# Words of a product kernel's weights fetched a pair ahead, and other first banks: a change to a one-core attention and MLP kernel

## The chip, the cores and the metric

The kernel runs on one core of a Trainium2 chip. The core has a matrix engine (PE, with its own weight loads, PEld), a vector engine (DVE), a scalar engine (ACT), a general engine (POOL, GpSimd) and a sync engine (SP). Each works through its own queue of instructions in order, and waits at an instruction until what that one needs is there. DMA transfers are issued by SP and by POOL. PE writes into PSUM banks, from which DVE and ACT read. The metric is the device time of one execution in microseconds (us); lower is better.

## What is computed

Four batches of chunked attention (8 heads, 768 tokens, head size 64; each chunk of 32 tokens sees 16 tokens to the left, 8 to the right and 8 memory slots), and behind it a mixer with a two-layer MLP:

```python
x = attn_out.transpose(0, 2, 1, 3).reshape(B, S, H * D)
h = x.transpose(0, 2, 1) @ U @ V
u = x + h.transpose(0, 2, 1)
out = u + np.maximum(u @ w_ch1, 0.0) @ w_ch2
```

w_ch1 is 512 x 2048, w_ch2 is 2048 x 512. All is float32; PE gets each operand as a high part and a remainder, three products for one.

## The kernel before

The batches follow one another. While PE does the MLP of one batch, the attention of the next is worked in between, a step at a time.

**Batch 0** goes through `both_blocks`: 32 units, each a first-layer step (`w1_step`) of 128 hidden channels for 384 tokens and, some units later, a second-layer step (`w2_step`). At its end `fold_both` turns the next batch's u (transposes on PE, L1363), adds and subtracts blocks of it (fold, L1373) and splits these into th and tl (L1378), the right-hand sides of batch 1.

**Batches 1 to 3** go through `fast`. There the first layer takes 16 blocks of hidden channels as 8 pairs p, and makes each pair for both halves of the tokens (blocks 0 and 1) by seven products in place of eight, after Strassen. `products(p)` issues seven products (n = 0 to 6) of six matmuls each into three PSUM banks, b1 (n = 0, 3, 6), b2 (n = 1, 4) and b3 (n = 2, 5). The first product on a bank starts it, and the later ones add to it, after the value that stood there has been read: b1 is copied by ACT at n = 0 (into ta, L1448) and n = 3 (into kept, L1454), b2 and b3 go into the sums ta and tb on DVE (n = 1: L1450, n = 2: L1452, n = 4: L1457, n = 5: L1459), and n = 6 into kept (L1461). ta and tb are one tile each, named part in the trace. `split_hidden` makes the hidden values hh (ACT) and hl (DVE, L1418); that of ta is the last reader of ta in a pair. Behind `products(p)` comes `first_block(p - 1)`, two second-layer steps for the first half of the tokens, except behind pairs 0 and 4, where `products(p + 1)` follows at once. Behind pair 3 eight blocks of the other half follow, the rest at the batch's end.

**The banks** b1 and b3 are from the pool ps_h, b2 from ps_a. ps_h has two buffers, ps_a three; ps_a is the pool of the attention. The add that brings the second layer into x (L1192) reads banks of both pools.

**The factors** s of the products are sums of blocks of w1. `prepare(p + 1)`, called ahead of `products(p)`, has POOL fetch two val tiles (256 KB each, L1335) from a copy in HBM and make five sums of them (L1341); two more factors are read straight from the words (mixed[p, 1], mixed[p, 3]). `build_factor` rounds each to a high part (ACT, L1410) and subtracts it for the remainder (DVE, L1411). The first four go into w1l buffers, of which there are four, and the others into three s buffers; they are built behind the products n = 2, 3, 5 and 6 of the pair before, in the code. val and sums are slot tiles, 13 in rotation, which the attention uses as well.

**Order.** The queues of PE, POOL and SP follow the code's order through the whole program. DVE and ACT follow it at first, and then an order that a scheduler lays down when the program is built. POOL's queue also holds the stores of u to HBM (xd<-xa, xd<-x), the loads of x back from there (`recall`, L1168) and the output stores (L1163).

Of the kernel before, what the change touches and what calls it, by code (L numbers as in the profile page):

```python
# [57 lines left out]
def chunk_attn_then_mixer_kernel(  # L58
# [13 lines left out]
    nc = tc.nc  # L72
# [39 lines left out]
    def slot(shape, dtype, name):  # L112
        return tk.tile(shape, dtype, name=name, tag="slot")
# [1131 lines left out]
    def both_blocks(following):  # L1245

        units = []
        for f in range(SPLIT + LEAD):
            if f < SPLIT:
                units.append((0, f, 0, f == 0, None))  # L1250
            if f >= LEAD:
                g = f - LEAD
                units.append((1, g, 1, g == 0, False if g == SPLIT - 1 else None))
        units += [(0, f, 0, False, True if f == NF - 1 else None) for f in range(SPLIT, NF)]
        units += [(1, f, 0, f == SPLIT, True if f == NF - 1 else None) for f in range(SPLIT, NF)]
        prev = []
        for n, (blk, f, where, begins, ends) in enumerate(units):
            while done[0] < min(2 * NF, 2 * f + 1 + (n > LATE)):
                advance(1)
                more_w()  # L1260
            if n == 2:
                head.close()
            let_go()
            solo = n >= 2 * SPLIT
            if n == 2 * SPLIT:
                paced.close()
            for blk_, m, *_ in units[n:n + AHEAD + 1]:
                if m >= SPLIT and blk_ == 1:
                    get_w1l(m)
            w1l = w1ls[f]  # L1270
            if f >= SPLIT or blk == 1:
                del w1ls[f]
            if n == 2 * SPLIT - SOON or 2 * SPLIT - LAID <= n < 2 * SPLIT - LAID + 2:
                place(1)
            serve(RATEL if n < 2 * SPLIT else RATES)
            if n > 2 * SPLIT:
                border()
            if n == 0:
                for c, g3 in rest[:2]:
                    join_uT1(turn_x1(c), c, g3)  # L1280
            if n == len(units) - 1:
                for m in range(3):
                    build_factor(0, m)
            hid_ = w1_step(0, blk, f, w1l)
            if n == len(units) - 2:
                prepare(0)
            if n == len(units) - 5:
                open_turned()
            if n == len(units) - 1:
                open_fast()  # L1290
                for m in range(3, len(PRODUCTS)):
                    build_factor(0, m)
            if n == 0:
                decode(2, 4)
                for c, g3 in rest[2:]:
                    join_uT1(turn_x1(c), c, g3)
                decode(1, 1)
                decode(2, 6)
                decode(1, 6)
                decode(3, 2)  # L1300
            for _ in range(RATE + (3 < n < 12)):
                advance(1)
                more_w()
            if n > 2 * SPLIT:
                border()
            if n >= len(units) - 3:
                following()
            prev.append((blk, f, where, begins, ends) + hid_)
            if solo or n % 2 == 0 or ends:
                while len(prev) > (not ends):  # L1310
                    while done[0] < 2 * prev[0][1] + 2:
                        advance(1)
                        more_w()
                    w2_step(0, *prev.pop(0))
# [12 lines left out]
    def border():  # L1327
        place(PLAN[at[0]])
        at[0] += 1

    def prepare(p):

        whole = [slot([P, NCK, P], F32, "val") for _ in range(2)]
        for side in range(2):
            nc.gpsimd.dma_start(out=whole[side], in_=val_d[2 * p + side])  # L1335
        mixed[p, 1], mixed[p, 3] = whole[1][:, 2:4, :], whole[0][:, 0:2, :]
        for m, (n, fa, ca, fb, cb, op) in enumerate(SUMS):
            if m % 2 == 0:
                two = slot([P, 2, 2, P], F32, "sums")
            a, b_ = (whole[f][:, 2 * c:2 * c + 2, :] for f, c in ((fa, ca), (fb, cb)))  # L1340
            nc.gpsimd.tensor_tensor(out=two[:, m % 2], in0=a, in1=b_, op=getattr(ALU, op))  # L1341
            mixed[p, n] = two[:, m % 2]
# [80 lines left out]
    def seven(b, kept, last):  # L1423
# [4 lines left out]

        def products(p):
            banks = [ps_h.tile([P, 512], F32, name="ps_h"), ps_a.tile([P, 512], F32, name="ps_a")]  # L1430
            banks.append(ps_h.tile([P, 512], F32, name="ps_h"))
            banks = [bank_[:, :TOK] for bank_ in banks]
            b1, b2, b3 = banks
# [52 lines left out]
    def fast(b, following):  # L1486
# [3 lines left out]
        for p in range(n):  # L1490
            if p + 1 < n or b + 1 < B:
                prepare((p + 1) % n)
            products(p)
            if p % (n // 2):
                first_block(p - 1)
            if p == n // 2 - 1:
                first_block(p)
                recall(b, 1)
                second_block(list(range(n)), False, fast_border)
# [77 lines left out]
```

## Time and profile before

| | |
|---|---|
| median of 3 runs | 653.23 us (651.63 to 653.72) |
| the profiled execution | 654.93 us |
| its span in the trace | 653.2 us |
| PE busy | 619.0 us (95%) |
| DVE busy | 458.8 us (70%) |
| ACT busy | 293.4 us (45%) |
| POOL busy | 189.9 us (29%) |
| granted clock of PE | 0.987 on average |

The span is the time from the first to the last instruction of the profiled execution; 1.7 us of that execution lie outside it. Busy time counts an engine's own operations. A bracket behind an operation in a timeline is the time that the engine sat idle before it, with what released it.

### The profile page before, as it was taken

The page shows a single profiled execution, that of the slowest core. Times are in us where ns is not written, and L with a number is a line of the kernel's source. Part 1 is how long each engine was busy: PE and PEld are TensorE (multiplying, and loading weights), DVE is VectorE, ACT ScalarE, POOL GpSimd, SP SyncE. Part 2 cuts the span into 40 slices and gives each one's busy share as a digit, 9 for nine tenths or more (in the row PEclk, how much of TensorE's full clock was granted, in tenths as well). Part 3 has the DMA queues.
Part 4 walks back from the last instruction along what each step waited for, and adds up shares of the span by engine and source line. Part 5 has one row for each costly group of instructions (what it writes and reads, how often), then busy time and mean ns, then how long its engine had stood idle before and what let it go on. Part 6 is the DMA issues. An engine that isn't in the chain of part 4 may idle for free.

```text
span 653.2 us, 15318 instructions
## 1 busy us (share of the span) xinstructions
PE 619.0 (95%) x6052; PEld 537.6 (82%) x6054; DVE 458.8 (70%) x983; ACT 293.4 (45%) x700; POOL 189.9 (29%) x294
## 2 busy tenths in 40 slices
PE   7687999999899999999999999999999999999997
PEld 6556999987786798878898898988798799889986
DVE  4875998889555988756676969766776966427542
ACT  4656776655223545533334545532333643314321
POOL 3520011000002764004631663003731564006400
PEclk9889999999898999999999999999999999999999
DMA  9996679655996239976211439942221442003411
GB/s 204 170 287 253 223 213 247 160 148 140 155 206 126 80 131 167 150 107 130 97 50 65 153 122 153 165 57 82 72 75 43 143 154 82 2 16 97 129 48 50
DMA packets 157082, 84.17 MB, mean 129 GB/s; under 512 B 128978, under 2 KB 143314, under 8 KB 157010
## 3 DMA queue, kind: packets, MB, share of 16 engines
q1 hardware_dynamic: 146034, 47.40, 36.2%
q0 software_dynamic: 10976, 35.79, 16.4%
q8 instruction: 48, 0.79, 0.5%
q14 instruction: 24, 0.20, 0.1%
HBM read 63.63 MB, written 19.40 MB: 127 GB/s over the span
## 4 chain that ended last, share of the span: by engine, by line
PE 59%; issue 18%; DVE 11%; DMA 6%; ACT 2%; POOL 2%; SPq 1%; POOLq 0%; DVEq 0%; ACTq 0%
PE ps_h L1442 17%; PE acc L1231 10%; PE ps_a L1442 7%; PE ps_h L1231 5%; PE acc L1236 5%; PE ps_h L1236 2%; PE ps_a L1231 2%; DVE tl L1378 2%; DMA vb<-in_v_dram 2%; DVE fold L1373 1%; PE ps_a L756 1%; PE ps_a L713 1%; PE ps_a L1236 1%; DMA val<-vald 1%; POOL vald L374 1%
## 5 line engine op out<-in xcount | busy, mean ns | idle before, releaser
L1341 POOL TENSOR_TENSOR sums<-val 128x256 f32<-128x256 f32 x120 | 98.0, 847 | 56.9 <-DMA val<-vald 43.9
L1231 PE MATMUL acc<-w,hh 128*128 128x512 f32 x366 | 98.0, 403 | 1.0 <-DVE w L382 1.0
L1442 PE MATMUL ps_h<-th,w1l 128*128 128x384 f32 x288 | 84.2, 344 | 6.5 <-DVE part L1459 5.0
L1231 PEld LDWEIGHTS acc<-w,hh 128*128 128x128 f32 x366 | 67.9, 190 | 16.2 <-issue 1.8
L1442 PEld LDWEIGHTS ps_h<-th,w1l 128*128 128x128 f32 x288 | 53.0, 188 | 12.1 <-ACT pT L747 3.6
L1418 DVE SCALAR_TENSOR_TENSOR hl<-kept,hh 128x384 fp32r<-128x384 f32 x48 | 28.8, 599 | 40.3 <-PE ps_a L1236 23.0
L1442 PE MATMUL ps_h<-th,s 128*128 128x384 f32 x192 | 52.8, 336 | 0.0
L1236 PE MATMUL acc<-w,hl 128*128 128x512 f32 x183 | 51.9, 392 | 0.0
L1442 PE MATMUL ps_h<-tl,w1l 128*128 128x384 f32 x144 | 49.0, 340 | 0.9 <-DVE tl L1378 0.9
L1417 ACT ACTIVATE hh<-kept 128x384 fp32r<-128x384 f32 x48 | 25.2, 526 | 54.0 <-PE ps_a L1231 29.2
L1231 PE MATMUL ps_h<-w,hh 128*128 128x512 f32 x156 | 43.4, 400 | 0.0
L1178 PE MATMUL ps_h<-uh,w1h 128*128 128x384 f32 x124 | 42.5, 349 | 0.8 <-ACT uh L1150 0.8
L1178 PE MATMUL ps_h<-ul,w1h 128*128 128x384 f32 x124 | 41.2, 340 | 0.0
L1236 PEld LDWEIGHTS acc<-w,hl 128*128 128x128 f32 x183 | 34.4, 189 | 7.8 <-issue 0.2
L1448 ACT COPY part<-ps_h 128x384 f32<-128x384 f32 x24 | 11.5, 480 | 62.8 <-PE ps_h L1442 54.6
L1231 PE MATMUL ps_a<-w,hh 128*128 128x512 f32 x132 | 37.9, 390 | 1.8 <-ACT hh L1184 1.8
L1163 POOL DMA_DIRECT2D xd<-x x9 | 4.9, 543 | 114.5 <-DVE x L1192 113.7
L1410 ACT CAST s<-sums 128x256 fp32r<-128x256 f32 x72 | 28.6, 402 | 17.1 <-PE ps_h L1442 13.7
L1411 DVE TENSOR_TENSOR w1l<-sums,w1l 128x256 fp32r<-128x256 f32 x48 | 25.4, 529 | 14.8 <-ACT w1l L1410 14.8
L1442 PEld LDWEIGHTS ps_h<-th,s 128*128 128x128 f32 x192 | 35.0, 188 | 0.0
L1231 PEld LDWEIGHTS ps_h<-w,hh 128*128 128x128 f32 x156 | 28.2, 188 | 5.7
L1184 ACT ACTIVATE hh<-ps_h 128x384 fp32r<-128x384 f32 x31 | 15.0, 487 | 38.7 <-PE ps_h L1178 38.7
(290 smaller groups left out, 1469.4 us busy)
## 6 DMA issues: line engine op xcount, KB each, us to landing
val<-vald POOLq DMA_DIRECT2D x48, 256.0 KB, 3.1
vb<-in_v_dram SPq DMA_DIRECT2D x23, 336.0 KB
rw<-in_moe_w_ch_dram SPq DMA_DIRECT2D x14, 512.0 KB
x<-xd POOLq DMA_DIRECT2D x27, 256.0 KB, 4.0
raw<-in_moe_w_ch_dram SPq DMA_DIRECT2D x20, 256.0 KB
kall<-in_k_dram SPq DMA_DIRECT2D x48, 96.0 KB
kall<-in_q_dram SPq DMA_DIRECT2D x48, 96.0 KB
out_dram<-x POOLq DMA_DIRECT2D x18, 256.0 KB, 3.0
```

Source lines behind the costliest of these rows:

```text
L1178: nc.tensor.matmul(out=ph[:, :TOK], lhsT=w[:, c, :], rhs=u[c], start=(m == 0), stop=(m + 1 == len(parts)),)
L1184: nc.scalar.activation(out=hh, in_=ph[:, :TOK], func=AF.Relu)
L1231: nc.tensor.matmul(out=acc[tt], lhsT=h[:, sl], rhs=w, start=(begins and m == 0), stop=False,)
L1236: nc.tensor.matmul(out=acc[tt], lhsT=hl[:, sl], rhs=w2h[f], start=False, stop=ends is not None)
L1341: nc.gpsimd.tensor_tensor(out=two[:, m % 2], in0=a, in1=b_, op=getattr(ALU, op))
L1378: nc.vector.tensor_tensor(out=tl[:, i:i + m, :, sl], in0=f32[n][:, 0:m], in1=th[:, i:i + m, :, sl].bitcast(F32), op=ALU.subtract,)
L1410: nc.scalar.copy(out=s[:, 0:2], in_=total)
L1411: nc.vector.tensor_tensor(out=s[:, 2:4], in0=total, in1=s[:, 0:2].bitcast(F32), op=ALU.subtract)
L1417: nc.scalar.activation(out=hh, in_=src, func=AF.Relu)
L1418: vpace[0] = nc.vector.scalar_tensor_tensor(out=hl, in0=src, scalar=0.0, in1=hh.bitcast(F32), op0=ALU.max, op1=ALU.subtract,)
L1442: nc.tensor.matmul(out=banks[at_], lhsT=w[:, wc, :], rhs=t[:, i, c, :], start=(n < 3 and m == 0), stop=(m + 1 == len(parts)), skip_group_c ...
L1448: nc.scalar.copy(out=ta, in_=b1)
```

## The change

There are three edits. The words of a pair go into fixed places, the last 512 of the 2048 words per partition of two of v's tiles (vb), which v leaves free, and no longer into slot tiles; so they have one buffer. The fetch is now a function, `fetch_words`, and is called two pairs ahead, behind `products(p)` for pair p + 2, so that pair p + 1's words have already been read. In pairs 0 and 4 the first two banks change places: b1 comes from ps_a and b2 from ps_h. And at the end of batch 0 the first words are fetched and summed in the sixth last unit, not in the second last; the second pair's words are fetched in the last one.

```diff
--- before.py
+++ after.py
@@ -1282,7 +1282,8 @@
                 for m in range(3):
                     build_factor(0, m)
             hid_ = w1_step(0, blk, f, w1l)
-            if n == len(units) - 2:
+            if n == len(units) - 6:
+                fetch_words(0)
                 prepare(0)
             if n == len(units) - 5:
                 open_turned()
@@ -1290,6 +1291,7 @@
                 open_fast()
                 for m in range(3, len(PRODUCTS)):
                     build_factor(0, m)
+                fetch_words(1)
             if n == 0:
                 decode(2, 4)
                 for c, g3 in rest[2:]:
@@ -1328,11 +1330,16 @@
         place(PLAN[at[0]])
         at[0] += 1
 
-    def prepare(p):
-
-        whole = [slot([P, NCK, P], F32, "val") for _ in range(2)]
+    whole = [
+        vb.rearrange("p i d -> p (i d)")[:, NX * D:NX * D + CH].rearrange("p (c f) -> p c f", c=NCK) for vb in vbs[:2]
+    ]
+
+    def fetch_words(p):
         for side in range(2):
             nc.gpsimd.dma_start(out=whole[side], in_=val_d[2 * p + side])
+
+    def prepare(p):
+
         mixed[p, 1], mixed[p, 3] = whole[1][:, 2:4, :], whole[0][:, 0:2, :]
         for m, (n, fa, ca, fb, cb, op) in enumerate(SUMS):
             if m % 2 == 0:
@@ -1428,6 +1435,8 @@
 
         def products(p):
             banks = [ps_h.tile([P, 512], F32, name="ps_h"), ps_a.tile([P, 512], F32, name="ps_a")]
+            if p % (NF // 4) == 0:
+                banks.reverse()
             banks.append(ps_h.tile([P, 512], F32, name="ps_h"))
             banks = [bank_[:, :TOK] for bank_ in banks]
             b1, b2, b3 = banks
@@ -1491,6 +1500,8 @@
             if p + 1 < n or b + 1 < B:
                 prepare((p + 1) % n)
             products(p)
+            if p + 2 < n or b + 1 < B:
+                fetch_words((p + 2) % n)
             if p % (n // 2):
                 first_block(p - 1)
             if p == n // 2 - 1:
```

Both kernels issue the same instructions, and PE's order stays. On SP two of v's loads for batch 3 now stand behind loads of k and q. Lines from 1331 on carry other numbers behind the change: L1442 becomes L1451, L1335 L1339, L1341 L1348, L1411 L1418, L1418 L1425, L1450 L1459, L1452 L1461, L1457 L1466, L1459 L1468, L1461 L1470, L1373 L1380, L1378 L1385.

PE, pair 0 and the start of pair 1 of batch 1, the first matmul of each product; a number behind a name is the allocation, and a new ps_h takes the bank of one of the two before it. Before:

```order
L1442 MATMUL ps_h_3208<-th_2839,w1l_3102 128x384 [waits Activation_49]
...
L1442 MATMUL ps_a_3209<-th_2839,w1l_3105 128x384 [waits PE_49,Activation_49]
...
L1442 MATMUL ps_h_3210<-th_2839,w1l_3108 128x384 [waits Activation_49]
...
L1442 MATMUL ps_h_3208<-th_2839,w1l_3134 128x384 [waits Activation_49]
...
L1442 MATMUL ps_a_3209<-th_2839,s_3137 128x384 [waits DVE_49]
...
L1442 MATMUL ps_h_3210<-th_2839,s_3140 128x384 [waits DVE_49]
...
L1442 MATMUL ps_h_3208<-th_2839,s_3143 128x384 [waits Activation_49]
...
L1442 MATMUL ps_h_3318<-th_2839,w1l_3234 128x384 [waits DVE_49]
...
L1442 MATMUL ps_a_3319<-th_2839,w1l_3254 128x384 [waits PE_49]
```

The same place now:

```order
L1451 MATMUL ps_a_3205<-th_2849,w1l_3100 128x384 [waits PE_49,Activation_49]
...
L1451 MATMUL ps_h_3204<-th_2849,w1l_3103 128x384 [waits Activation_49]
...
L1451 MATMUL ps_h_3206<-th_2849,w1l_3106 128x384 [waits Activation_49]
...
L1451 MATMUL ps_a_3205<-th_2849,w1l_3132 128x384 [waits Activation_49]
...
L1451 MATMUL ps_h_3204<-th_2849,s_3135 128x384 [waits DVE_49]
...
L1451 MATMUL ps_h_3206<-th_2849,s_3138 128x384 [waits DVE_49]
...
L1451 MATMUL ps_a_3205<-th_2849,s_3141 128x384 [waits Activation_49]
...
L1451 MATMUL ps_h_3312<-th_2849,w1l_3230 128x384 [waits DVE_49]
...
L1451 MATMUL ps_a_3313<-th_2849,w1l_3250 128x384 [waits PE_49]
```

Pair 0's products 0, 3 and 6 have moved to ps_a and 1 and 4 to ps_h; pair 1 (3318 and 3319, now 3312 and 3313) has its banks as before, and its first, from ps_h, can take the bank of pair 0's b2, which now is one of the last two from there.

POOL, pair 4 of batch 1: x loads and xd stores of the batch's first half, and the words of pair 5 (vald_140, 141) and 6 (142, 143). Before:

```order
L1168 DMA x<-xd_3_149 128x512
L1168 DMA x<-xd_4_150 128x512
L1168 DMA x<-xd_5_151 128x512
L1163 DMA xd_3_149<-x 128x512
L1163 DMA xd_4_150<-x 128x512
L1163 DMA xd_5_151<-x 128x512
L1335 DMA val<-vald_140 128x512
L1335 DMA val<-vald_141 128x512
L1341 TENSOR_TENSOR sums<-val 128x256 x5
L1335 DMA val<-vald_142 128x512
L1335 DMA val<-vald_143 128x512
```

The same place now:

```order
L1339 DMA vb_104<-vald_140 128x512
L1339 DMA vb_105<-vald_141 128x512
L1168 DMA x<-xd_3_149 128x512
L1168 DMA x<-xd_4_150 128x512
L1168 DMA x<-xd_5_151 128x512
L1163 DMA xd_3_149<-x 128x512
L1163 DMA xd_4_150<-x 128x512
L1163 DMA xd_5_151<-x 128x512
L1348 TENSOR_TENSOR sums<-vb_104 128x256
L1348 TENSOR_TENSOR sums<-vb_104,vb_105 128x256
L1348 TENSOR_TENSOR sums<-vb_105 128x256
L1348 TENSOR_TENSOR sums<-vb_104,vb_105 128x256
```

The words of pair 5 have moved ahead of the loads and the stores, and their sums follow the stores directly.

DVE, pair 4 of batch 1: the reads of pair 4's banks (n = 1, 2, 4, 5), the softmax of an attention step (rs) and the remainders of pair 5's factors. Before:

```order
L1450 TENSOR_TENSOR part_3132<-ps_a,part_3132 128x384
L736 TENSOR_REDUCE rs<-pt 128x6
L1452 TENSOR_TENSOR part_3133<-ps_h,part_3132 128x384
L736 TENSOR_REDUCE rs<-pt 128x6
L737 TENSOR_SCALAR rs<-rs 128x12
L738 RECIPROCAL rs<-rs 128x12
L1411 TENSOR_TENSOR w1l<-sums,w1l 128x256
L1411 TENSOR_TENSOR w1l<-val,w1l 128x256
L1418 SCALAR_TENSOR_TENSOR hl<-ps_a,hh 128x384
L1457 TENSOR_TENSOR part_3133<-part_3133,ps_a 128x384
L1411 TENSOR_TENSOR w1l<-sums,w1l 128x256
L1459 TENSOR_TENSOR part_3132<-ps_h,part_3132 128x384
```

The same place now:

```order
L1459 TENSOR_TENSOR part_3130<-ps_h,part_3130 128x384
L1418 TENSOR_TENSOR w1l<-sums,w1l 128x256
L1418 TENSOR_TENSOR w1l<-vb_105,w1l 128x256
L736 TENSOR_REDUCE rs<-pt 128x6
L1461 TENSOR_TENSOR part_3131<-ps_h,part_3130 128x384
L736 TENSOR_REDUCE rs<-pt 128x6
L1418 TENSOR_TENSOR w1l<-sums,w1l 128x256
L1418 TENSOR_TENSOR w1l<-vb_104,w1l 128x256
L737 TENSOR_SCALAR rs<-rs 128x12
L1425 SCALAR_TENSOR_TENSOR hl<-ps_h,hh 128x384
L1466 TENSOR_TENSOR part_3131<-part_3131,ps_h 128x384
```

The first four remainders have moved up, from behind the softmax to places around the first two reads.

DVE, end of batch 0: the last part of u (xa), the first folds, and the first remainders of batch 1. Before:

```order
L1067 TENSOR_TENSOR g_2940<-ps_a,g_2940 32x512
L1083 TENSOR_TENSOR xa<-ps_a,xa 128x512 x2
L1185 SCALAR_TENSOR_TENSOR hl<-ps_h,hh 128x384
L1083 TENSOR_TENSOR xa<-ps_a,xa 128x512 x4
L1373 TENSOR_TENSOR fold<-ps_a,fold 128x256 x5
L1378 TENSOR_TENSOR tl<-fold,th 128x4x128
L1378 TENSOR_TENSOR tl<-fold,th 128x2x128
L1378 TENSOR_TENSOR tl<-fold,th 128x4x128 x2
L1411 TENSOR_TENSOR w1l<-sums,w1l 128x256
L1411 TENSOR_TENSOR w1l<-val,w1l 128x256
L1185 SCALAR_TENSOR_TENSOR hl<-ps_h,hh 128x384
```

The same place now:

```order
L1418 TENSOR_TENSOR w1l<-sums,w1l 128x256
L1067 TENSOR_TENSOR g_2950<-ps_a,g_2950 32x512
L1083 TENSOR_TENSOR xa<-ps_a,xa 128x512 x2
L1185 SCALAR_TENSOR_TENSOR hl<-ps_h,hh 128x384
L1083 TENSOR_TENSOR xa<-ps_a,xa 128x512
L1418 TENSOR_TENSOR w1l<-vb_105,w1l 128x256
L1083 TENSOR_TENSOR xa<-ps_a,xa 128x512 x3
L1380 TENSOR_TENSOR fold<-ps_a,fold 128x256 x5
L1385 TENSOR_TENSOR tl<-fold,th 128x4x128
L1385 TENSOR_TENSOR tl<-fold,th 128x2x128
L1385 TENSOR_TENSOR tl<-fold,th 128x4x128 x2
L1185 SCALAR_TENSOR_TENSOR hl<-ps_h,hh 128x384
```

Two remainders have moved ahead of the folds, one of them in between the additions to xa.

## Rows read from the trace of the kernel before

**Rows 1.** Page, part 1: engine, busy us, share of the span, instructions.

```profile
PE 619.0 (95%) x6052; PEld 537.6 (82%) x6054; DVE 458.8 (70%) x983; ACT 293.4 (45%) x700; POOL 189.9 (29%) x294
```

**Rows 2.** Waits of PE: who waits <- for whom, us in total, times, longest.

```profile
PE ps_h L1442 <- DVE part L1459: 5.0, 5, 1.7
PE ps_a L756 <- DMA vb<-in_v_dram: 4.2, 3, 2.1
...
PE ps_h L1442 <- DVE x L1192: 1.0, 2, 0.5
...
PE ps_h L1442 <- DVE tl L1378: 0.9, 2, 0.5
...
PE ps_a L1442 <- DVE tl L1378: 0.7, 1, 0.7
...
PE ps_h L1442 <- ACT part L1448: 0.3, 1, 0.3
```

**Rows 3.** Timeline, PE, batch 2, pairs 0 to 1: start, us, operation [idle <- releaser].

```profile
374.34 0.41 PE L1442 MATMUL ps_h<-th,w1l 128*128 128x384 f32 x1 [0.51 <-DVE x L1192]
...
381.43 0.51 PE L1442 MATMUL ps_h<-th,s 128*128 128x384 f32 x2
382.70 0.45 PE L1442 MATMUL ps_h<-th,w1l 128*128 128x384 f32 x1 [0.76 <-DVE part L1459]
```

**Rows 4.** Timeline, DVE, same stretch of batch 2.

```profile
380.89 0.54 DVE L1457 TENSOR_TENSOR part<-part,ps_a 128x384 f32<-128x384 f32 x1
...
382.11 0.54 DVE L1459 TENSOR_TENSOR part<-ps_h,part 128x384 f32<-128x384 f32 x1
...
383.86 1.09 DVE L1418 SCALAR_TENSOR_TENSOR hl<-part,hh 128x384 fp32r<-128x384 f32 x1
```

**Rows 5.** Timeline, PE, pairs 4 to 5 of batch 1, then of batch 2.

```profile
307.81 0.82 PE L745 MATMUL ps_a<-ident,pt 128*128 128x128 f32 x6
310.34 0.41 PE L1442 MATMUL ps_h<-th,w1l 128*128 128x384 f32 x1 [1.72 <-DVE part L1459]
...
458.72 0.41 PE L1442 MATMUL ps_h<-th,w1l 128*128 128x384 f32 x1 [1.49 <-DVE part L1459]
```

**Rows 6.** Timeline, POOL, pair 4 of batch 1.

```profile
299.07 1.90 POOL L1163 DMA_DIRECT2D xd<-x  x3 [37.91 <-DVE x L1192]
301.04 1.15 POOL L1335 DMA_DIRECT2D val<-vald  x2
305.57 3.87 POOL L1341 TENSOR_TENSOR sums<-val 128x256 f32<-128x256 f32 x5 [3.39 <-DMA val<-vald]
```

**Rows 7.** Timeline, DVE, pair 4 of batch 1.

```profile
306.78 0.50 DVE L1411 TENSOR_TENSOR w1l<-sums,w1l 128x256 fp32r<-128x256 f32 x1 [1.48 <-ACT w1l L1410]
307.21 0.96 DVE L1411 TENSOR_TENSOR w1l<-val,w1l 128x256 fp32r<-128x256 f32 x1
...
309.02 0.71 DVE L1411 TENSOR_TENSOR w1l<-sums,w1l 128x256 fp32r<-128x256 f32 x1
309.65 0.54 DVE L1459 TENSOR_TENSOR part<-ps_h,part 128x384 f32<-128x384 f32 x1
310.12 0.41 DVE L1411 TENSOR_TENSOR w1l<-val,w1l 128x256 fp32r<-128x256 f32 x1
```

**Rows 8.** The tile val, all its transfers from issue on.

```profile
DMA to landing us min/median/max: 2.8/3.1/4.4
```

**Rows 9.** Timeline, DVE, end of batch 0.

```profile
210.22 3.31 DVE L1378 TENSOR_TENSOR tl<-fold,th 128x512 fp32r<-128x512 f32 x4
...
217.75 2.21 DVE L1378 TENSOR_TENSOR tl<-fold,th 128x512 fp32r<-128x512 f32 x4
```

**Rows 10.** POOL's stores; PE's wait; a stretch (DMA share, GB/s last).

```profile
177.24 1.81 POOL L1163 DMA_DIRECT2D out_dram<-x  x3 [22.03 <-DVE x L1192]
...
181.22 1.15 PE L756 MATMUL ps_a<-vb,pT 64*32 64x64 f32 x94 [1.30 <-DMA vb<-in_v_dram]
...
160.00:180.00 20.00, 16.69 (x260) 14.13 (x259) 12.34 (x31) 6.41 (x16) 1.62 (x3) 0.91 1.00 158
```

## The prediction

> **What bounds the kernel now.** I read the page first. The matrix engine is busy for 619.0 of 653.2 us [rows 1], so little can be won that is not one of its waits. Next I read the list of its waits by line and releaser [rows 2]. Most lines there belong to the head of the program and to batch 0, which the diff leaves alone. Those that bear on the change are four: the seven products (L1442) waiting for a vector add, L1459, five times, 5.0 us; for x, L1192, twice, 1.0 us; for the scalar engine's copy, L1448, once, 0.3 us; and for tl, L1378, three times, 0.9 + 0.7 us. Then I looked at each place in the timelines. The profiled execution took 654.93 us against a median of 653.23; its span is 653.2. I count in its microseconds and take the sum off the median. A measurement of this kernel can tell about 0.3%, or 2.0 us, from no change.
>
> A wait costs more than its bracket says. In [rows 3] the two matmuls that start at 381.43 come 0.175 us apart, so the next was due at 381.78; it started at 382.70. That is 0.92 us lost for a bracket of 0.76: 0.16 us more for the restart. I add 0.16 to each.
>
> So the four lines hold 5.0 + 5 x 0.16 = 5.8, 1.0 + 2 x 0.16 = 1.3, 0.46, and 1.6 + 3 x 0.16 = 2.1 us. Together 9.7 us: no more than that can be won.
>
> **First bank from the attention's pool.** Pairs 0 and 4 are followed by the next pair at once, with no second-layer step between. Before, all of b1 and b3 came from ps_h (two buffers), and the next pair's first bank had to be the bank of b3, free only after L1459. In batch 2 L1459 starts at 382.11 and PE goes on at 382.70 [rows 3, 4]. Now b1 is in ps_a, b2 in ps_h, and the next pair's first bank is b2's, free after the add that is L1457 today. L1457 starts at 380.89 and takes 0.54: 381.43, which is 0.35 us before the 381.78 at which PE wants it [rows 3, 4]. The three waits from pair 0 to 1 are what is left of the 5.0 once 1.72 and 1.49 for pairs 4 to 5 are taken off [rows 2, 5]: 1.8 + 3 x 0.16 = 2.3 us. What comes due next is ta. PE starts pair 1 0.9 us sooner; its first copy into ta must wait for hl<-part, and its fourth product for that copy. Before, hl ran 383.86 to 384.95 [rows 4]. Giving the copy behind it the 0.54 us of an add, it ends at 385.5, and product 4 was wanted at 382.70 + 3 x 1.05 = 385.85: less than 0.4 us to spare, which is less than the 0.9 gained. But hl took 1.09 there, twice the adds around it [rows 4], since POOL's sums ran beside it. The words of pair 2 are now asked for only when pair 1's fourth factor is built, around 380.1, so with 3.1 us of landing [rows 8] the sums start near 383.3 and not 380.4. I expect hl to end near 384, which gives 0.5 us to spare, and none if the sums meet it. I take **2.1 us**, bounds 0.9 (each place gives half of it back) and 2.3.
>
> Pair 0 itself: its first bank was ps_h, still being read by x<-ps_h, so PE lost 0.51 + 0.16 = 0.67 us at 374.34 in batch 2, and as much in batch 3 [rows 2, 3]. A ps_a bank is long free there, and ps_h is now wanted 1.05 us later, when x<-ps_h is over. **1.3 us**, bounds 1.0 and 1.3.
>
> **Words a pair ahead.** From pair 4 to 5 PE lost 1.72 and 1.49 us plus two restarts, 3.5 us, in batches 1 and 2 [rows 5]. Followed back in batch 1: L1459 starts at 309.65, behind one w1l subtraction, L1457, hl and two more w1l that start with 306.78, after 1.48 us of idle for the scalar engine's cast [rows 7]. The cast waited for the first sum, and POOL's sums could start only at 305.57, after 3.39 us of idle for the words [rows 6]. The words were asked for at 301.04, behind the xd stores, for which POOL had stood 37.91 us. Now the words lie in v's tiles before those stores, so the sums start when the stores are issued, 299.07 + 1.90 = 301.0, 4.5 us sooner, and end near 304.9. The scalar engine casts as each w1l buffer is set free by pair 4's products: seven of 6 x 0.175 = 1.05 us that end at 307.81, so the first four end at 301.5, 302.6, 303.6 and 304.7 [rows 5]. In the new order of the vector engine at pair 4 (shown under the change) two w1l stand directly behind the first part add, and two more behind the second. My walk with 0.41 to 0.55 us each puts hl at 306.8 and the add that frees the bank at 307.4 to 307.9. PE has six transposes of 0.82 us in all behind the products and wants the bank at 308.5. So 0.5 us to spare, less what the sums stretch. Beside the sums one w1l took 0.96 and one 0.71, clear of them one took 0.41 [rows 7]; two such in this window are 0.85 us more, and leave 0.3 us of wait. I take 0.4 us as what remains at each place: 3.5 - 0.8 = **2.7 us**, bounds 1.6 and 3.5. In batch 3 the same lateness shows as L1448's 0.46 us: **0.4**, bounds 0 and 0.46.
>
> In those rows the operations with one input in PSUM (L1457 at 0.54, L1459 at 0.54) kept their length beside the sums, and those with both in SBUF (w1l, hl<-part) were stretched by 0.30 to 0.55 us [rows 4, 7]. The Trainium skill, SBUF — State Buffer, "Who interferes with whom", says the same and more: a vector instruction with two SBUF inputs and a GpSimd one that reads SBUF lock each other out for a whole instruction, whichever comes second. The rows agree on who is hit, not on a whole sum (3.87 / 5 = 0.77) each time. By the page, moving the sums ahead on to four w1l would cost up to 4 x 0.77 = 3.1 us in place of my 0.85, and pairs 4 to 5 would keep all of their waits: a gain of 3.8 in place of 6.5 in all.
>
> What the change costs here. The words have one buffer, not a rotating slot, so the fetch for pair p + 2 stands on POOL behind the fourth factor of pair p + 1 (DVE) and POOL's own last sum; queued behind it are the x loads, the xd and the output stores. The fourth factor is ready some 5.3 us into a pair (four products, 4.2, a cast and a subtraction, about 0.5 each); with 3.1 us of landing and 0.8 for the first sum it is 9.2 us. Pair p + 2's sums are first looked for three products into pair p + 1, at 7.35 + 3.15 = 10.5 us where no second-layer step lies between, and later where one does. That leaves 1.3 us at the short crossings. One place is tighter: in pair 5 of batches 1 and 2 the scalar engine's cast of pair 6's first factor now stands ahead of the copy that frees PE's fourth product. Fetch 306.6, landed 309.8, sum 310.5, cast 310.9, copy 311.4; PE wants it at 308.5 + 3.15 = 311.6. So 0.2 us to spare at the median landing and 1.1 us of wait at the longest of 4.4 [rows 8]. I take **-0.1** for both, bounds 0 and -2.2. The x loads of a batch's start, queued behind such a fetch, have some 3 us to spare, which hides them. Two of v's loads for batch 3 now stand behind k's and q's on SP; PE's three waits for v are all in batch 0, the last until 181.22 [rows 2, 10], so I count them at nothing.
>
> **First sums four units ahead.** The vector engine runs with hardly a gap from 207.8 to 228, and PE waits for tl three times there [rows 2]. Beside POOL's first sums four tl took 3.31 us, later four took 2.21 [rows 9]. With the sums four units sooner the 1.1 us goes, and two w1l go ahead of the folds. But the next fold waits for transposes, and the next hl for a first-layer step, at PE's pace, so of this some 0.5 us, about half, can reach the end. The order at the end of batch 0 shows one w1l between the xa adds, for which PE's transposes wait: it can take half of an op's 0.41 back. **0.3 us**, bounds -0.4 and 0.8. The first words are now fetched right after the output stores that end at 179.05, while PE waits for v until 181.22 [rows 10]. Half a megabyte (0.524 MB) at the 158 GB/s that the DMA engines moved while they were all busy is 3.3 us, if all of it went ahead of v; v's loads were issued earlier. **-0.2**, bounds 0 and -3.3.
>
> **Sum:** 2.1 + 1.3 + 2.7 + 0.4 - 0.1 + 0.3 - 0.2 = 6.5 us off 653.23: **646.7 us**. By itself this case spans 645.0 (0.9 left of the 9.7) to 648.5.
>
> **Rivals.**
> 1. The banks come sooner, and the two chains behind them take half back. Sums beside hl leave 0.5 us of wait at each of the six crossings (3.0), and pairs 4 to 5 wait 0.9, not 0.4 (1.0): 650.7. For it: the 1.09 us of hl [rows 4], L1448's wait in batch 3 [rows 2]. Against it: the sums move away from that hl.
> 2. The first words push v's load back by 2.8 us, most of that half megabyte: 649.5 (6.5 - 2.8 = 3.7). For it: PE waits for v three times already, 4.2 us [rows 2]. Against: it is asked for last.
> 3. Slower: single-buffered words come too late. Every microsecond beyond the spare time stalls the cast, and behind it the copy and PE's fourth product, at four short crossings with 1.3 us to spare and two with 0.2. With landings of 6.0 us (2.9 over the median) that is 4 x 1.6 + 2 x 2.7 = 11.8 us against 6.5 won: 658.5. It decides from 5.1 us, where 4 x 0.7 + 2 x 1.8 = 6.4. The longest of 48 landings was 4.4 [rows 8], which speaks against it.
> 4. It does nothing: the second half of pair 5 or the attention chain ends at the same time, and PE waits there for what it gained: 653.
>
> **How the numbers follow.** My forecast 0.64, the first rival 0.16, the second 0.08, the third 0.05, the fourth 0.07. The range goes from 644.0, nearly all of the 9.7, to 651.0, which takes in the first two rivals. Faster by over 0.3% (under 651.3): 0.64 + 0.12 of the first + 0.08 = 0.84; within: 0.04 + 0.06 = 0.10; slower: 0.06.
>
> **What would show it.** Right: L1459's successor gone from PE's waits at pairs 0 to 1, under 0.5 us at pairs 4 to 5; POOL's sums of pair 5 start right behind the xd stores; PE starts pair 0 with no wait for x. Wrong: a new wait of the products for the L1448 copy (first rival or, with a POOL idle for the words longer than 3 us before it, the third); the wait for v after 179.6 longer than 1.3 us (second).

## The result and the profile after

The changed kernel takes 646.72 us in the median of 11 runs, the kernel before 653.83 beside it: a ratio of 0.9895, with a 95% interval of 0.9867 to 0.9923. That is 5.0 to 8.7 us less; the forecast was 6.5 less, 646.7 us. The profiled execution has a span of 644.7 us (before: 653.2).

The page of the changed kernel, its first part (busy us, share, count), against [rows 1]:

```profile
span 644.7 us, 15308 instructions
...
PE 616.5 (96%) x6052; PEld 536.5 (83%) x6054; DVE 450.4 (70%) x983; ACT 293.3 (45%) x700; POOL 186.1 (29%) x294
```

PE's waits of the changed kernel from batch 1 on (us in total, times, longest), against [rows 2]:

```profile
PE ps_h L1451 <- DVE tl L1385: 0.7, 2, 0.5
PE ps_h L1451 <- DVE part L1461: 0.5, 2, 0.2
PE ps_h L1451 <- ACT part L1457: 0.4, 2, 0.2
```

The 5.0 us for the add L1459 and the 1.0 for x are gone. Two waits of 0.2 us for an add stand in the list, L1461, which is L1452 of before (the read at n = 2), and two for the copy at n = 0. The waits for tl have gone from three to two.

The crossing from pair 0 to 1 in batch 2, of PE, then DVE, then ACT, against [rows 3, 4]:

```profile
376.36 0.51 PE L1451 MATMUL ps_a<-th,s 128*128 128x384 f32 x2
376.70 0.34 PE L1451 MATMUL ps_h<-th,w1l 128*128 128x384 f32 x1
```

```profile
375.82 0.54 DVE L1466 TENSOR_TENSOR part<-part,ps_h 128x384 f32<-128x384 f32 x1
...
378.22 0.55 DVE L1425 SCALAR_TENSOR_TENSOR hl<-part,hh 128x384 fp32r<-128x384 f32 x1
```

```profile
378.85 0.48 ACT L1457 COPY part<-ps_h 128x384 f32<-128x384 f32 x1 [1.06 <-DVE hl L1425]
```

L1466 is the add that was L1457. It ends at 376.36, and PE takes the bank at 376.70 without a wait: 0.34 us to spare. hl<-part is back at 0.55 us from 1.09, and the copy behind it ends at 379.33, half a microsecond before PE's fourth product of pair 1 at 376.70 + 3.15 = 379.85. Both spare times are those of the forecast (0.35 and 0.5).

The stage from the first product of batch 1 to the end took 653.2 - 223.6 = 429.6 us before and 644.7 - 222.1 = 422.6 now, 7.0 us less. The other 1.5 us between the two profiled spans lie ahead of it, in the head and in batch 0.

### Pairs 4 to 5

Here something is left. POOL in pair 4 of batch 1, against [rows 6]:

```profile
295.75 1.90 POOL L1163 DMA_DIRECT2D xd<-x  x3 [29.83 <-DVE x L1192]
297.67 0.75 POOL L1348 TENSOR_TENSOR sums<-vb 128x256 f32<-128x256 f32 x1
...
304.52 1.11 POOL L1339 DMA_DIRECT2D vb<-vald  x2 [3.34 <-DVE rs L737]
```

The sums follow the xd stores at once, as meant. PE there, and DVE, against [rows 5] and [rows 7]:

```profile
302.05 0.51 PE L1451 MATMUL ps_h<-th,s 128*128 128x384 f32 x2
302.79 0.44 PE L1451 MATMUL ps_h<-th,s 128*128 128x384 f32 x1 [0.23 <-DVE part L1461]
303.07 0.34 PE L1451 MATMUL ps_h<-tl,s 128*128 128x384 f32 x1
...
304.98 0.82 PE L745 MATMUL ps_a<-ident,pt 128*128 128x128 f32 x6
305.55 0.42 PE L1451 MATMUL ps_h<-th,w1l 128*128 128x384 f32 x1
...
308.47 0.52 PE L1451 MATMUL ps_h<-th,w1l 128*128 128x384 f32 x2
309.15 0.44 PE L1451 MATMUL ps_h<-th,w1l 128*128 128x384 f32 x1 [0.17 <-ACT part L1457]
```

```profile
299.50 0.56 DVE L1459 TENSOR_TENSOR part<-ps_h,part 128x384 f32<-128x384 f32 x1
299.97 1.50 DVE L1418 TENSOR_TENSOR w1l<-sums,w1l 128x256 fp32r<-128x256 f32 x1
301.40 0.41 DVE L1418 TENSOR_TENSOR w1l<-vb,w1l 128x256 fp32r<-128x256 f32 x1
...
302.19 0.54 DVE L1461 TENSOR_TENSOR part<-ps_h,part 128x384 f32<-128x384 f32 x1
...
304.33 0.53 DVE L1466 TENSOR_TENSOR part<-part,ps_h 128x384 f32<-128x384 f32 x1
```

The bank is no longer the matter. L1466 ends at 304.86 and PE goes from the six transposes (304.98) to pair 5 at 305.55 with no bracket. But PE lost 0.39 us before product n = 5 (302.79, where 302.40 was due), waiting for L1461, since product n = 5 adds to the bank which L1461 reads. L1461 stood behind one w1l that took 1.50 us beside the sums. The matmul behind the stalled one comes late as well, at 303.07, 0.28 us after it where 0.175 is usual: 0.10 us more. The same 0.10 stands behind the stalls between products before, and the prediction's 0.16 for a restart leaves it out. The second loss is at 309.15, 0.34 us, for the copy at n = 0. ACT:

```profile
308.31 0.41 ACT L1417 CAST w1l<-sums 128x256 fp32r<-128x256 f32 x1 [1.49 <-POOL sums L1348]
308.63 0.47 ACT L1457 COPY part<-ps_h 128x384 f32<-128x384 f32 x1
```

The copy stands behind the cast of pair 6's first factor, and that waited 1.49 us for the sum. Batch 2 shows the same two losses, 0.39 and 0.38 us.

### The profile page after: what moved, and what is told of

It is laid out like the page before. It is cut to its first block, busy times and chain, and to the rows that moved or that the text cites. A ratio compares the mean times of both kernels' runs of the same rounds, so it can differ in the third digit from the quotient of the medians.

```text
span 644.7 us, 15308 instructions
## 1 busy us (share of the span) xinstructions
PE 616.5 (96%) x6052; PEld 536.5 (83%) x6054; DVE 450.4 (70%) x983; ACT 293.3 (45%) x700; POOL 186.1 (29%) x294
## 4 chain that ended last, share of the span: by engine, by line
PE 71%; issue 10%; DMA 7%; DVE 7%; POOL 2%; ACT 1%; SPq 1%; DVEq 0%; POOLq 0%; ACTq 0%
PE ps_h L1451 17%; PE acc L1231 12%; PE ps_a L1451 8%; PE ps_h L1231 6%; PE acc L1236 6%; PE ps_h L1178 3%; PE ps_a L1231 3%; PE ps_h L1236 3%; PE ps_a L756 2%; PE ps_a L713 2%; PE ps_a L1236 1%; DMA raw<-in_moe_w_ch_dram 1%; PE ps_h L1223 1%; DMA rw<-in_moe_w_ch_dram 1%; PE ps_a L1370 1%
## 5 line engine op out<-in xcount | busy, mean ns | idle before, releaser
L1451 PE MATMUL ps_h<-th,w1l 128*128 128x384 f32 x264 | 76.5, 343 | 0.5 <-ACT part L1457 0.4
L1348 POOL TENSOR_TENSOR sums<-vb,vb 128x256 f32<-128x256 f32 x72 | 58.6, 826 | 4.2 <-DMA vb<-vald 1.6
L1425 DVE SCALAR_TENSOR_TENSOR hl<-kept,hh 128x384 fp32r<-128x384 f32 x48 | 28.8, 599 | 40.1 <-PE ps_a L1236 22.8
L1348 POOL TENSOR_TENSOR sums<-vb 128x256 f32<-128x256 f32 x48 | 37.7, 785 | 57.9 <-DMA vb<-vald 48.8
L1451 PE MATMUL ps_h<-th,s 128*128 128x384 f32 x192 | 53.4, 337 | 0.5 <-DVE part L1461 0.5
L1451 PEld LDWEIGHTS ps_h<-th,w1l 128*128 128x128 f32 x264 | 48.6, 188 | 3.8 <-issue 1.7
L1418 DVE TENSOR_TENSOR w1l<-sums,w1l 128x256 fp32r<-128x256 f32 x48 | 28.3, 590 | 33.4 <-ACT w1l L1417 33.4
L1339 POOL DMA_DIRECT2D vb<-vald x48 | 26.3, 549 | 85.6 <-issue 42.1
L1451 PE MATMUL ps_h<-tl,w1l 128*128 128x384 f32 x132 | 44.9, 340 | 0.7 <-DVE tl L1385 0.7
L1451 PEld LDWEIGHTS ps_h<-th,s 128*128 128x128 f32 x192 | 35.1, 188 | 1.1 <-DVE part L1461 1.1
L1451 PE MATMUL ps_a<-th,w1l 128*128 128x384 f32 x120 | 36.0, 340 | 0.0
```

The source lines that it names most:

```text
L1418: nc.vector.tensor_tensor(out=s[:, 2:4], in0=total, in1=s[:, 0:2].bitcast(F32), op=ALU.subtract)
L1425: vpace[0] = nc.vector.scalar_tensor_tensor(out=hl, in0=src, scalar=0.0, in1=hh.bitcast(F32), op0=ALU.max, op1=ALU.subtract,)
L1451: nc.tensor.matmul(out=banks[at_], lhsT=w[:, wc, :], rhs=t[:, i, c, :], start=(n < 3 and m == 0), stop=(m + 1 == len(parts)), skip_group_c ...
```

## The experiments

All times are against runs of the kernel before on the same chip. Counted from start to start, as in the prediction, PE lost at the places in question (us; stalls of 0.1 us and more, without the 0.10 for the matmul behind; one profiled execution each):

| place | before | changed | banks alone | words alone | first sums alone | changed, no banks | changed, held back |
|---|---|---|---|---|---|---|---|
| pair 0 to 1, three times | 2.3 | 0 | 1.2 | 1.6 | 2.0 | 1.6 | 0 |
| pair 0, for x, twice | 1.3 | 0 | 0 | 0 | 0.7 | 0 | 0 |
| pairs 4 and 5, batches 1 and 2 | 3.5 | 1.5 | 2.8 | 1.4 | 3.8 | 1.4 | 0 |
| pairs 4 and 5, batch 3 | 0.8 | 0.3 | 0.7 | 1.1 | 0.6 | 1.1 | 0.3 |
| tl, end of batch 0 | 2.1 | 1.0 | 2.7 | 1.2 | 1.4 | 1.1 | 1.1 |
| sum | 10.1 | 2.8 | 7.3 | 5.2 | 8.5 | 5.1 | 1.4 |
| median, us | 653.7 | 646.7 | 649.9 | 647.8 | 652.9 | 650.1 | 644.3 |
| ratio | | 0.9895 | 0.9938 | 0.9924 | 1.0005 | 0.9939 | 0.9868 |

Before and the changed kernel differ by 7.3 us in the sum and by 7.0 in the length of the stage, so the table holds nearly all of the gain. A second profiled execution of the changed kernel gives a sum of 3.0 in place of 2.8, so a difference of 0.2 between columns tells nothing. As a check that needs no threshold, pairs 4 and 5 of batches 1 and 2 take, from the first matmul to the start of the last, 34.3 us before, 32.6 in the changed kernel, 32.7 with the words alone and without the banks, and 30.7 held back.

The 2.7 us for tl with the banks alone are not explained by that edit. A part is the clock: in that execution PE was granted a clock of 0.50 (1.2 GHz) from 225.2 to 228.0, behind two waits for tl of 1.30 and 0.75 us, and its matmuls came 0.32 us apart; in the kernel before and the changed one the granted clock of this stretch was 1.00. That makes 0.3 of the 2.7, and 1.1 us more that stand in no row; what is left above the 2.1 of before is open. The medians alone, with intervals of 0.2 to 0.4% to either side, don't rank the variants; the places do.

### Banks alone

```diff
             banks = [ps_h.tile([P, 512], F32, name="ps_h"), ps_a.tile([P, 512], F32, name="ps_a")]
+            if p % (NF // 4) == 0:
+                banks.reverse()
             banks.append(ps_h.tile([P, 512], F32, name="ps_h"))
```

> The kernel before with the exchange of the first two banks in pairs 0 and 4 alone; words and first sums as before. My theory: the three waits from pair 0 to 1 and the two for x at pair 0 go (2.3 + 1.3 us), and at pairs 4 to 5 the bank is free after the add behind hl, at 309.1 in the old trace's time, not after the next one at 310.2, so the wait there falls from 1.9 to about 0.8 us: 1.1 us each, 5.5 us in all less 0.3 for a copy that then comes late; ratio 0.992. Rival: the banks win only what stands at pairs 0, 3.6 us (ratio 0.9945), since at pairs 4 to 5 it is the late words that hold everything; then the wait there stays near 1.7 us each.

Measured: 0.9938 (0.9913 to 0.9963), 4.1 us. The PE waits of its trace, then DVE and ACT at pair 0 to 1 of batch 2:

```profile
PE ps_h L1444 <- ACT s L1410: 1.9, 2, 1.2
PE ps_a L1444 <- DVE tl L1378: 1.3, 1, 1.3
PE ps_h L1444 <- ACT part L1450: 1.0, 3, 0.4
```

```profile
378.65 0.54 DVE L1459 TENSOR_TENSOR part<-part,ps_h 128x384 f32<-128x384 f32 x1
...
381.49 1.09 DVE L1418 SCALAR_TENSOR_TENSOR hl<-part,hh 128x384 fp32r<-128x384 f32 x1
```

```profile
382.66 0.48 ACT L1450 COPY part<-ps_h 128x384 f32<-128x384 f32 x1 [1.84 <-DVE hl L1418]
```

No wait for a bank is left at pair 0 to 1. But PE reaches pair 1 sooner and then waits for the copy at its fourth product, three times (1.0 us by the brackets, 1.2 from start to start): POOL's sums still run beside hl, 1.09 us, and the copy can start only at 382.66. This is the first rival of the prediction, and it is what the exchange alone would have met. At pairs 4 to 5 the loss falls from 3.5 to 2.8, not by 1.1 at each place. The words came later in this execution: the sums start 5.13 and 4.62 us behind the issue of the words (304.84 - 299.71, 451.58 - 446.96), before 4.53 and 4.31, and the add that frees the bank moves with them; why they landed later is open. Another 0.25 us at each place is a new wait for the copy. So both sides of this expectation missed: the fall at pairs 4 to 5 is between the theory's and the rival's.

### Words alone

```diff
             hid_ = w1_step(0, blk, f, w1l)
-            if n == len(units) - 6:
+            if n == len(units) - 2:
                 fetch_words(0)
...
-            if p % (NF // 4) == 0:
-                banks.reverse()
```

(against the changed kernel)

> The changed kernel without the exchange of banks, and with the first sums in the second last unit as before: the words a pair ahead alone. My theory: pairs 4 to 5 lose their late sums, and 0.4 us of wait for the bank is left besides the two small stalls of about 0.35 us that the changed kernel has there, so 2.4 us of 3.5 are won; 0.4 in batch 3; from pair 0 to 1 the sums no longer lie beside the adds, which gives back 0.4 us each: 4.0 us in all, ratio 0.994. The waits for x at pair 0 stay. Rival: without the banks the words win nothing at pair 0 to 1, and only 1.7 us at pairs 4 to 5: 2.1 us, ratio 0.997.

Measured: 0.9924 (0.9898 to 0.995), 5.0 us. PE's waits:

```profile
PE ps_h L1449 <- DVE part L1466: 2.0, 4, 0.9
PE ps_h L1449 <- DVE tl L1385: 0.5, 1, 0.5
PE ps_h L1449 <- DVE part L1459: 0.4, 2, 0.2
```

Three of the four waits for L1466 (L1459 of before) are at pair 0 to 1, 0.35 us each; before they were 0.36, 0.76 and 0.71. The adds themselves keep their 0.54 us; what was stretched beside the sums is the subtraction between the two adds. DVE in batch 2, before and then in this run:

```profile
381.36 0.83 DVE L1411 TENSOR_TENSOR s<-sums,s 128x256 fp32r<-128x256 f32 x1
```

```profile
374.80 0.42 DVE L1418 TENSOR_TENSOR s<-sums,s 128x256 fp32r<-128x256 f32 x1
```

The fourth wait, 0.9 us, is at pairs 4 to 5 of batch 3, and is longer than what was lost there before (1.1 against 0.8 in the table). The wait for x at pair 0 is gone, with ps_h still the first bank. That the prediction had not seen. In the kernel before, the end of batch 1 has, POOL first and then DVE:

```profile
365.30 5.09 POOL L1341 TENSOR_TENSOR sums<-val 128x256 f32<-128x256 f32 x5 [1.96 <-DVE tl L1378]
...
366.41 2.37 DVE L1378 TENSOR_TENSOR tl<-fold,th 128x512 fp32r<-128x512 f32 x2
```

and in this one:

```profile
355.89 1.04 POOL L1348 TENSOR_TENSOR sums<-vb 128x256 f32<-128x256 f32 x1 [3.56 <-DVE tl L1385]
...
361.17 1.28 DVE L1385 TENSOR_TENSOR tl<-fold,th 128x512 fp32r<-128x512 f32 x2
```

The sums ran just ahead of the batch's end and stretched two tl to 2.37 us and two hl beside them; now they start at 355.89, 12 us ahead of the first product of batch 2 (367.85), in place of 9 (374.34), and the later tl take 1.28 (two hl still take 1.08 and 1.09). DVE begins with x<-ps_h 1.2 us ahead of that product; before, it began only when PE was ready for it (373.51). The first sums alone show the same link by accident: at the end of batch 2 POOL idled 0.46 us behind the first of the five sums, the two tl beside them took 1.82 us in place of 2.37, and the wait for x fell from 0.67 to 0.13 us from start to start. At pairs 4 and 5 1.4 us are left: 0.40 and 0.38 before product n = 5, 0.15 twice for the bank, and 0.18 and 0.12 for the copy at n = 0.

### First sums alone

```diff
             hid_ = w1_step(0, blk, f, w1l)
-            if n == len(units) - 2:
+            if n == len(units) - 6:
                 prepare(0)
```

(against the kernel before)

> The kernel before with its first fetch and sums in the sixth last unit of batch 0, nothing else. My theory: the waits for tl fall from 2.1 us to about 1.0, and the transposes behind xa come 0.35 us later: 0.7 us faster, ratio 0.999, which the times alone can't tell from 1; the trace decides. Rival: the words' transfers meet v's loads there, and PE's wait for v around 180 grows by up to 2.8 us: ratio 1.003.

Measured: 1.0005 (0.9977 to 1.0032). The loss to tl is 1.4 us in place of 2.1, and the transposes behind xa start 0.34 us later, as expected; 0.3 us remain of the 0.7 expected, which the times can't show. PE's wait for v near 180 was 1.29 us from start to start (before 1.51), so nothing of the rival. And the words alone, with the first sums late, show 1.2 us there, against 1.0 of the whole change with its 0.34 behind xa: beside the words this edit is worth nothing that these traces show.

### The change without the banks

```diff
-            if p % (NF // 4) == 0:
-                banks.reverse()
```

(against the changed kernel)

> The changed kernel with the exchange of banks undone. My theory: the gains of e2_words and e3_first together, 4.7 us, ratio 0.993, so the banks are worth some 2 us on top of the words, while they are worth 5.5 alone. Rival: the edits add up, and without the banks the kernel gains only 7.1 - 5.5 = 1.6 us, ratio 0.9975.

Measured: 0.9939 (0.9918 to 0.9961), 4.0 us. By the places 5.1 us are lost, 2.8 with the banks: 2.3 us for the exchange on top of the words, as the theory had it (some 2). Alone the exchange is worth 2.8 by the table, not the 5.5 that the theory took from the first expectation, so the edits nearly add up (2.8 and 4.9 for the words alone, 7.3 together). Its gain on top of the words is in pair 0 to 1 (1.6) and batch 3 (0.8). At pairs 4 and 5 of batches 1 and 2 it moves the loss and saves nothing (1.4 us without it, 1.5 with it): the wait for the bank goes, and the stall for the copy grows, since PE reaches pair 5 sooner.

### Sums that read nothing

```diff
-            nc.gpsimd.tensor_tensor(out=two[:, m % 2], in0=a, in1=b_, op=getattr(ALU, op))
+            nc.gpsimd.memset(two[:, m % 2], 0.25)
```

(against the changed kernel)

> The changed kernel with the five sums of a pair replaced by fills of the same size: the general engine writes as much but reads nothing, so the factors hold a constant. My theory: in pair 4 of batches 1 and 2 the w1l subtraction that took 1.50 us in the changed kernel takes its 0.41 again, and the PE stall of 0.39 us before product n = 5, which waits for the add behind it, goes; the same holds for hl and s elsewhere. Some 0.8 us in all on PE. Rival: the stretch comes from writing, or from the queue of the general engine, not from reading; then the subtraction stays over 0.9 us.

The tile sums in the changed kernel (min, median and max in ns of the operations that read it), then in this one:

```profile
L1418 DVE TENSOR_TENSOR w1l<-sums,w1l x48: 404/428/1808, 195.5 to 600.8; 128x256 fp32r<-128x256 f32 x48
```

```profile
L1348 POOL MEMSET sums<- x120: 305/331/337, 178.9 to 593.9; 128x256 f32 x120
...
L1418 DVE TENSOR_TENSOR w1l<-sums,w1l x48: 411/425/427, 195.8 to 601.1; 128x256 fp32r<-128x256 f32 x48
```

The subtraction that reached 1808 ns stays at 411 to 427, and both stalls of pairs 4 and 5 are gone. The fills are shorter than the sums (0.33 us, not 0.75), so this alone could be a matter of less overlap. Where they do overlap, POOL first and then DVE:

```profile
305.13 1.34 POOL L1348 MEMSET sums<- 128x256 f32 x5
...
305.10 0.36 DVE L1418 TENSOR_TENSOR s<-sums,s 128x256 fp32r<-128x256 f32 x1
...
305.84 0.41 DVE L1418 TENSOR_TENSOR s<-sums,s 128x256 fp32r<-128x256 f32 x1
```

the two s (both inputs in SBUF) beside the five fills took 0.36 and 0.41 us: no stretch. So it is the sums' reading, or their length, that stretches; in these two, writing beside it does not. The scheduler's order changed with the fills, and one stall of 1.49 us for a copy came up elsewhere; the one time, 646.43 us, shows no gain.

### Words that come later

```diff
-            nc.gpsimd.dma_start(out=whole[side], in_=val_d[2 * p + side])
+            for _ in range(2):
+                nc.gpsimd.dma_start(out=whole[side], in_=val_d[2 * p + side])
```

(against the changed kernel)

> The changed kernel with each of the two words' transfers of a pair issued twice, the same data to the same place, so that the words come about 1.1 us later (two more issues of 0.55) or more. My theory of the tight place: in pair 5 of batches 1 and 2 the stall of 0.34 us before product n = 3, behind a copy that stands behind the cast of pair 6's first factor, grows by the delay to 1.4 us or more each, 2.2 us in all; the crossings with 1.3 us to spare show nothing or little. Rival (the late words decide everywhere): new stalls for the words at four more crossings, over 5 us in all, and the kernel is back at 652 or worse.

Measured: 708.75 us in one run, 62 more than the changed kernel. The delay was not 1.1 us. POOL in batch 1:

```profile
255.43 0.57 POOL L1340 DMA_DIRECT2D vb<-vald  x1 [1.25 <-issue]
262.05 1.07 POOL L1340 DMA_DIRECT2D vb<-vald  x2 [6.05 <-DMA vb<-vald]
267.53 0.54 POOL L1340 DMA_DIRECT2D vb<-vald  x1 [4.42 <-DMA vb<-vald]
268.09 0.73 POOL L1349 TENSOR_TENSOR sums<-vb 128x256 f32<-128x256 f32 x1
```

The second transfer to the same place waits on POOL until the first has landed, 6.05 and 4.42 us here, so a pair's words take 12.7 us from the first issue to the first sum, in place of 3.0 (304.52 to 307.55 in the changed kernel). PE's largest waits, and ACT at the worst place:

```profile
PE ps_a L745 <- ACT pt L734: 24.7, 4, 10.7
PE ps_h L1452 <- DVE part L1462: 4.2, 5, 2.8
```

```profile
268.86 0.40 ACT L1418 CAST w1l<-sums 128x256 fp32r<-128x256 f32 x1 [5.93 <-POOL sums L1349]
...
273.22 0.52 ACT L734 ACTIVATE pt<-pt 128x384 f32<-128x384 f32 x1
```

Not all of the 62 us are waits: PE's busy time is 631.8 us against 616.5, 15.3 more, for the same instructions. The clock that it was granted was 0.96 on average from the first product on, against 1.00 in the changed kernel; from 267.4 to 277.7, for one, it was 0.50 (1.2 GHz), and it fell to that in the wait of 10.7 us below. The largest part of the waits, 24.7 us, is not at the products. ACT stood 5.93 us at the first cast, for the sum, and behind the casts stand the exponentials of the next batch's attention (pt, L734), for which PE's transposes waited 10.7 us. So late words do decide here, as the third rival said, but by another path than the one that it priced. The run does not tell what 1.1 us would have done.

### Three instructions held back

```diff
+            if (p, n) == (6, 0):
+                held.enter_context(tc.issue_after(behind[0].ins))
             nc.scalar.copy(out=s[:, 0:2], in_=total)
...
+            if p == 5 and n in (0, 1):
+                held.enter_context(tc.issue_after(behind[2].ins))
             nc.vector.tensor_tensor(out=s[:, 2:4], in0=total, in1=s[:, 0:2].bitcast(F32), op=ALU.subtract)
```

(in build_factor of the changed kernel; behind[0] is the copy at n = 0, behind[2] the add at n = 2)

> The changed kernel with three instructions held back in the scheduler's order: in pair 4 the subtractions of pair 5's first two factors stand behind the add of n = 2, and in pair 5 the cast of pair 6's first factor behind the copy of n = 0. My theory: the stalls of 0.39 and 0.34 us in batches 1 and 2 go, 1.2 to 1.5 us, ratio 0.987 to before and 0.998 to the changed kernel; the words' lateness has no other path to PE there. Rival: the held-back subtractions delay hl and the bank's release, and the time is the same or worse.

Measured: 644.34 us, 0.9868 (0.9832 to 0.9904); the changed kernel again in the same group 646.72 us, 0.9904 (0.9869 to 0.9939).

> The changed kernel again, to set the others of this group against it: ratio 0.989 to before, as measured first.

PE's waits:

```profile
PE ps_h L1458 <- DVE tl L1385: 0.8, 2, 0.5
PE ps_a L745 <- ACT pt L734: 0.2, 1, 0.2
PE ps_a L1458 <- DVE part L1466: 0.2, 1, 0.2
```

All four stalls of pairs 4 and 5 in batches 1 and 2 are gone, 1.5 us; two new ones in the first half of batch 1 (transposes behind a softmax exponential, and a product behind an add, 0.2 us each by the brackets, 0.7 from start to start) take some of it back. From the first product to the end it takes 421.0 us, against 422.6 for the changed kernel. The intervals of the two ratios overlap, so by the times alone it is not shown to be faster than the changed kernel; against the kernel before it is.

## Why the prediction was right, and where it was not

**The time** was right, and so was the reading behind it: PE is the bound, and only its waits could be won. Of 9.7 us of waits counted, 6.5 were to go; 7.3 went of the 10.1 in the table, which takes in one wait more. Each wait between products cost 0.26 us more than its bracket, not 0.16, which changes the sizes a little and no place.

**Pair 0 to 1**: 2.1 forecast, 2.3 measured. Both halves of the argument are borne out: the bank is free in time, and hl is no longer stretched, which keeps the copy from becoming the next wait. The banks alone show what the second half was worth, 1.2 us.

**Pair 0, for x**: 1.3 forecast and 1.3 measured, for a cause that was enough but not the only one. The bank from ps_a is one way to lose the wait, and the earlier sums at the batch's end are another; either alone does it. The step that failed is that the prediction did not follow where the first words of the next batch move the sums of its pair 1.

**Pairs 4 to 5**: 2.7 forecast, 2.0 measured (3.5 - 1.5; the length of the two pairs fell by 1.8). The prediction gave 0.4 us of wait to each place, and put it at the bank. The bank costs nothing: it is free at 304.86, and PE wants it near 305.55. What is left is 0.7 to 0.8 at each place and stands at two others. One of the two, before product n = 5, cost 0.39 us, so that the 0.4 came true in size, but by luck; the whole shortfall against 2.7 is the other one, the tight place below. The walk through DVE's new order followed only the add that frees the bank; it left out that product n = 5 adds to the bank that the add of n = 2 must have read, and that this add now stands behind two w1l. The stretch was taken too small as well: 0.55 us was the largest in the rows, 1.09 was met (1.50 for 0.41), about as long as one and a half sums. The rule of the Trainium skill that was weighed there (SBUF — State Buffer, "Who interferes with whom": the two contend for an exclusive lock, taken there as a wait of the later one for the whole of the other) was nearer to that one operation than the rows of before were: one sum is 0.75 us. Its total, all the waits kept, was not met, as only one of the four w1l was hit so.

**The tight place** in pair 5 was named rightly, the cast ahead of the copy, and sized too low: -0.1 for both places, 0.7 measured (0.34 + 0.38). The landing was as forecast, 3.0 us from issue to sum. The term that was off is the fetch: the prediction had it at 306.6, 6.3 us behind the start of pair 4 (300.33 before), and POOL issued it at 304.52, 7.5 us behind that start (297.01), after 3.34 us of idle for the vector engine, where the fourth factor's subtraction came only at 303.45, behind the w1l of 1.50 us. Holding the cast back behind the copy, and the two subtractions behind the add, takes all four stalls away.

**Batch 3**: 0.4 forecast, 0.5 measured (0.8 to 0.3), but not by the words, to which the prediction put it down: with the words alone the loss grows to 1.1, for the bank, and only the exchange with them brings it to 0.3.

**First sums**: 0.3 forecast. Measured 1.1 less for tl and 0.3 more behind xa, 0.7 to 0.8; but the words alone give as much, so the edit that was credited does not carry it. The first words did not collide with v: -0.2 forecast, nothing measured. PE's waits for v at L756 are 3.2 us in the changed kernel's trace against the 4.2 of [rows 2]. The words themselves were late there, 8.2 us from the issue to the first sum (177.91 to 186.12), with nothing waiting for them.

**The rivals.** The first is in the main what happens with the banks alone. Its sign, a new wait of the products for the copy, stands in the changed kernel too, but only at pairs 4 to 5, 0.4 us by the brackets, and with 1.92 us of idle for the words on POOL, under the 3 that were to mark the third. The second did not happen. Of the third it is shown, at a delay of some 10 us, that late words stall the cast; its path to PE was another, and its price per microsecond is not shown. The fourth fell.

Term by term: 2.3 + 1.3 + 2.0 + 0.5 + 0.7 = 6.8 us from the places, against 2.1 + 1.3 + 2.7 + 0.4 + 0.3 - 0.1 - 0.2 = 6.5 forecast. That the two agree so well rests on errors that cancel: -0.6 at pairs 4 to 5 (2.0 against 2.7 - 0.1) and +0.6 for tl and v together. The sum was right in part by luck.

## What to carry to other kernels

When an engine's wait goes, look at every later use of the same banks and tiles in that stretch, not only at the one that was waited for: here the matmuls that go on accumulating waited for the read between them. Work of a second engine that is moved sooner can win by what it no longer runs beside, and not only by being ready: here 0.7 us at pair 0 to 1 and the wait for x. And where casts wait for a single-buffered load, ask what stands behind them in their engine's queue: the load's lateness goes to whoever waits for that. Where many small stalls take the place of a large one, compare the length of the whole stretch as well.

## What the runs showed of the hardware

A subtraction with both inputs in SBUF took 1.50 us at one place and 1.81 at the most beside the general engine's sums, and 0.41 clear of them; the adds with one input in PSUM kept 0.53 to 0.56 in all rows shown. Fills by the general engine did not stretch the two such operations that ran beside them (0.36 and 0.41 us). A product that waited cost PE its bracket and 0.16 us, and the matmul behind it another 0.10. A second transfer into a tile that a first was still filling held the general engine's queue for 4.4 and 6.1 us in the rows shown. PE's granted clock fell to 0.50 in a wait of 10.7 us, and was 0.50 as well behind two waits of 1.30 and 0.75 us close together.
